# Moving the x tile of the odd groups and the four weight tiles to SBUF addresses that are multiples of 2048 bytes

## The chip, the cores and the metric

The kernel runs on one core of one Trainium2 chip. The metric is the device time of one execution in microseconds; the number to be compared is the median of several runs.

## What is computed

Two stages follow each other. The first is a linear attention with decay, for 4 batches, 8 heads, 768 time steps and a head width of 48:

```python
for t in range(S):
    kt, vt, rt, wt = (k[:, :, t], v[:, :, t], r[:, :, t], w[:, :, t])
    cur = np.einsum('bhd,bhe->bhde', u[None] * kt, vt)
    y[:, :, t] = np.einsum('bhd,bhde->bhe', rt, state + cur)
    state = wt[:, :, :, None] * state + np.einsum('bhd,bhe->bhde', kt, vt)
```

Its output, 3072 tokens of 384 values, goes through a two-layer network with 2048 hidden units; `h`, `g` and the output are in float32:

```python
h = x @ w_in
g = h * (1.0 / (1.0 + np.exp(-1.702 * h)))
return g @ w_out
```

## The kernel before

**Tiling.** The 3072 tokens are 24 chunks of 128. The function `chunk` does the attention of one chunk with small matmuls on TensorE (lines L251, L267, L283, L284, L295, L308, L315) and elementwise work on VectorE and ScalarE. Four chunks make a group of 512 tokens; there are six groups, 0 to 5. The result of a chunk is written, in two parts, into the group's `x` tile: `split` (L192) puts a rounded value (`hi`, L193, ScalarE) and what the rounding lost (`lo`, L194, VectorE). An `x` tile is 128 partitions by 2 parts by 4 blocks of 512 columns in a 4-byte type, so each block is 2048 bytes of every partition and the tile is 16384. Of the four blocks three hold the 384 features; the fourth is a staging block whose rows `fill_x` (L333) copies to their places by DMA.

**The two products.** The weights are kept the same way, as rounded part and rest: `wih`, `wil` for the first layer, `woh`, `wol` for the second, each 128 partitions by 16 hidden slices by 384 columns, 24576 bytes of a partition. A task is one group (or half a group, in group 0) and one of 16 hidden slices `f`. For a task `first_product` does nine matmuls: three feature blocks by three terms, L345 (`wih` with the rounded x), L346 (`wih` with the rest of x) and L347 (`wil` with the rounded x). The weight slice is 128 columns (512 bytes) and is loaded into the array by a LDWEIGHTS of its own; the streamed operand is one block of `x`, 512 columns, read from its first byte to its last. `gelu` turns the sum into `gh` and `gl` (L356 and L357 on ScalarE, L358 on VectorE). `second_product` does nine matmuls likewise: L371 (`woh`, `gh`), L372 (`wol`, `gh`), L373 (`woh`, `gl`), streamed operand `gh` or `gl`, 2048 bytes each. In group 0 most tasks cover 256 columns.

**Order.** The order of everything is written out by hand: `RAMP` and `rest` give a list of tokens, and `do` emits them. In the string, `g`, `h` and `y` stand for first product, gelu and second product of a task; the second product comes two tasks behind the first. The attention of the next chunks is put between the tasks of groups 0 to 4; group 5 has next to none left beside it.

**Where tiles lie.** `new_x` (L383) takes the `x` tile of an even group from the pool `mo` and that of an odd group from the pool `late`:

```python
return (mo if i % 2 == 0 else pools["late"]).tile([P, 2, NP, WIDE], F32R, tag="x", name="x", bufs=1)
```

`late` is opened (L413) when the last weight has been converted, in the memory that the pool `su` with the weights' staging tiles leaves. The pool `cp`, opened first, holds the constants, the four weight tiles, and `acc`, a small tile of sums for a test at the end. The start addresses in each partition, as the program is built, and what is left of them after division by 2048:

```
tile                       bytes    start before  mod 2048
wih, wil, woh, wol         24576 each   22272 ...     1792 (all four)
acc                          240       120576         1792
x of groups 0, 2, 4 (mo)   16384       120832            0
gh (3 buffers), gl (3)      2048 each  141312 ...        0 (all six)
x of groups 1, 3, 5 (late) 16384       194496         1984
rk_t (2 buffers, late)      3072 each  210880      1984, 960
ob (3 buffers, late)        2048 each  217024 ...     1984
```

Since 24576 is 12 times 2048 and a weight slice is 512 bytes, the slices of a weight tile start in turn at 1792, 256, 768 and 1280 mod 2048; one in four runs over a multiple of 2048. Every block of an odd group's `x` starts 64 bytes ahead of a multiple of 2048 and runs over it; no block of an even group's does, and no `gh` or `gl`.

Of the kernel before, what the change touches and what calls it, by code (L numbers as in the profile page):

```python
# [8 lines left out]
F32 = mybir.dt.float32  # L9
F32R = mybir.dt.float32r  # L10
# [9 lines left out]
DM, DFF = H * D, 2048  # L20
NTOK = B * S
P = 128
# [8 lines left out]
NF = DFF // P  # L31
# [44 lines left out]
y38 a13 y39 h40 x11 g41 h41 m12  # L76
"""
WIDE = 512
assert sum(CHUNKS) == NT


@with_exitstack
def rwkv_ffn_kernel(ctx: ExitStack, tc, wkr, vp, vrk, ub, w_in, w_out, masks, vt, uc, out):
# [3 lines left out]
    cp = ctx.enter_context(tc.tile_pool(name="cp", bufs=1))  # L87
# [34 lines left out]

    A.activation(at.tile([P, 1], F32, tag="s", name="junk", bufs=2), after[:, 0:1], AF.Gelu_apprx_sigmoid)

    wih, wil, woh, wol = (cp.tile([P, NF, DM], F32R, name=x) for x in ("wih", "wil", "woh", "wol"))
    acc = cp.tile([P, 2 * NT + 2 * NL], F32, name="acc")
    G.memset(acc, 0.0)

    loaded, state, pools = {}, {}, {}

# [22 lines left out]
    def fetch(i, pool):  # L153

        s, which = divmod(i, 2)
        if s >= NL:
            return
        n = SL // NL
        st = staged[i] = pool.tile([P, n, 2 * NF * DM // SL], I32, tag="st", name="st", bufs=3)
        src = (w_in, w_out)[which][s * n : (s + 1) * n].bitcast(I32)  # L160
        if which == 0:
            for i, (dst, rows) in enumerate(X_ROWS):
                (nc.sync, G)[i % 2].dma_start(st[dst], src[:, rows].rearrange("n p w -> p n w"))
        else:
            nc.sync.dma_start(st, src.rearrange("n p w -> p n w"))

    def convert(i, pool, clamp):

        s, which = divmod(i, 2)
        hi, lo = (wih, wil) if which == 0 else (woh, wol)  # L170
        n = NF * DM // NL
        hi, lo = (x.rearrange("p f m -> p (f m)")[:, s * n : (s + 1) * n] for x in (hi, lo))
        st = staged.pop(i)
        c = pool.tile([P, n], I32, tag="c", name="c", bufs=2)
        w = st.rearrange("p k (n two) -> p (k n) two", two=2)
        l, h = w[:, :, 0], w[:, :, 1]
        cf = c.bitcast(F32)
        sums = {} if clamp else dict(accum_out=acc[:, 2 * NT + i : 2 * NT + i + 1])
        A.activation(l, l.bitcast(U32), AF.Copy, scale=L_SCALE)
        A.activation(cf, h.bitcast(F32), AF.Abs, scale=W_SHIFT, **sums)  # L180
        yield
        V.scalar_tensor_tensor(h, h, -(2 ** 31), l, op0=ALU.bitwise_and, op1=ALU.bitwise_or)
        if clamp:
            V.tensor_scalar(cf, cf, W_MAX, None, op0=ALU.min)
        V.scalar_tensor_tensor(c, c, 3, h, op0=ALU.logical_shift_left, op1=ALU.bitwise_or)
        yield
        A.copy(hi, cf)
        yield
        V.tensor_tensor(lo, cf, hi.bitcast(F32), op=ALU.subtract)  # L189
        yield  # L190
# [136 lines left out]
    def fill_x(x, c0, c1):  # L327

        for m in range(NM):
            for i, dst in enumerate((D, R2)):  # L330
                j = 32 * m + 16 * i
                j += 0 if j < D else HB - D
                (nc.sync, G)[i].dma_start(  # L333
                    x[dst : dst + 16, :, m, c0:c1].bitcast(F32), x[j : j + 16, :, NM, c0:c1].bitcast(F32)
                )
# [3 lines left out]
    def first_product(j, task):  # L339
        i, c0, c1, f = task  # L340
        cs = slice(c0 * C, c1 * C)
        ph = ps_h.tile([P, WIDE], F32, tag="ph", name="ph")[:, 0 : (c1 - c0) * C]
        for c in range(NM):
            h_, l_ = (w[:, f, c * P : (c + 1) * P] for w in (wih, wil))
            T.matmul(ph, h_, xs[i][:, 0, c, cs], start=c == 0, stop=False)  # L345
            T.matmul(ph, h_, xs[i][:, 1, c, cs], start=False, stop=False)  # L346
            T.matmul(ph, l_, xs[i][:, 0, c, cs], start=False, stop=c == NM - 1)  # L347
        parts[j] = ph

    def gelu(j, task):  # L350
        i, c0, c1, f = task
        ph, n = parts[j], (c1 - c0) * C
        gf = mo.tile([P, WIDE], F32, tag="gf", name="gf")[:, 0:n]
        gh = mo.tile([P, WIDE], F32R, tag="gh", name="gh", bufs=LAG + 1)[:, 0:n]
        gl = mo.tile([P, WIDE], F32R, tag="gl", name="gl", bufs=LAG + 1)[:, 0:n]
        A.activation(gh, ph, AF.Gelu_apprx_sigmoid, scale=1.0 / W_SCALE)  # L356
# [4 lines left out]
    def second_product(j, task):  # L361
# [3 lines left out]
        if first:  # L365
            po[i] = [ps_o.tile([P, WIDE], F32, tag=f"po{m}", name=f"po{m}") for m in range(NM)]
        for m in range(NM):
# [7 lines left out]
    def store(i, start, N):  # L375

        for m, o in enumerate(po.pop(i)):
            ob = pools["late"].tile([P, WIDE], F32, tag="ob", name="ob", bufs=3)[:, 0:N]
            A.activation(ob, o[:, 0:N], AF.Copy, scale=1.0 / W_SCALE)
# [7 lines left out]
    with tc.manual_schedule():  # L387
        early = ExitStack()
        su = early.enter_context(tc.tile_pool(name="su", bufs=1))
        where = [(i, col) for i, n in enumerate(CHUNKS) for col in range(n)]  # L390
        starts = [sum(CHUNKS[:i]) for i in range(len(CHUNKS))]
        last = {}
        for j, task in enumerate(TASKS):
            last[task[0]] = j
        running, told = {}, {}

        def piece(kind, i):

            if (kind, i) not in running:
                running[kind, i] = {  # L400
                    "l": load, "a": chunk, "m": measures.get, "w": lambda i: convert(i, su, False)
                }[kind](i)
            next(running[kind, i])

        def do(token):
            kind, i = token[0], int(token[1:] or 0)
            told[token] = told.get(token, 0) + 1
            if kind in "lamw":
                piece(kind, i)
                if kind == "w" and all(told.get(f"w{n}") == 4 for n in range(2 * NL)):  # L410
                    early.close()
                    pools["late"] = fast.enter_context(tc.tile_pool(name="late", bufs=2))
            elif kind == "f":  # L413
                fetch(i, su)
            elif kind == "x":
                group, col = where[i]
                if i == 1:
                    fill_x(xs[group], 0, 2 * C)
                elif i == 3:
                    fill_x(xs[group], 2 * C, 4 * C)  # L420
                elif col == CHUNKS[group] - 1:
                    fill_x(xs[group], 0, (col + 1) * C)
            elif kind == "u":
                nc.sync.dma_start(u_sb, ub)
            elif kind == "M":
                A.dma_start(hm[0:D], masks[0:D])
                A.dma_start(hm[HB:R2], masks[D:R])
            elif kind == "g":
                first_product(i, TASKS[i])
            elif kind == "h":  # L430
                gelu(i, TASKS[i])
            elif kind == "y":
                second_product(i, TASKS[i])
                group = TASKS[i][0]
                if i == last[group]:
                    store(group, starts[group] * C, CHUNKS[group] * C)

        def rest():

            begins = []  # L440
            for t, (i, col) in enumerate(where):
                n = len([x for x in TASKS if x[0] == i - 1])
                begins.append(last.get(i - 1, -1) + 1 - BEFORE - round((CHUNKS[i] - 1 - col) * n / CHUNKS[i]))
            ramp = dict(told)
            for j in range(FIRST, len(TASKS) + LAG):
                for post in range(2):
                    if post and j < len(TASKS):
                        yield f"g{j}"
                        yield f"h{j}"
                    for t, begin in enumerate(begins):  # L450
                        for kind, step, half in PARTS:
                            token = f"{kind}{t + 2 * (kind == 'l')}"
                            if (step + begin, half) > (j, post) or kind == "l" and t + 2 >= NT:
                                continue
                            if ramp.get(token, 0):
                                ramp[token] -= 1
                            elif (step + begin, half) == (j, post):
                                yield token
                if j - LAG >= 0 and f"y{j - LAG}" not in told:
                    yield f"y{j - LAG}"  # L460

        for token in RAMP.split():
            do(token)
        for token in rest():
            do(token)
# [15 lines left out]
    with tc.If(n < full):  # L481
# [5 lines left out]
        with tc.tile_pool(name="gp", bufs=1) as gp, tc.tile_pool(name="ob", bufs=2) as ob, tc.For_i(0, B, 1) as b:  # L487
            pools["late"] = ob
            xg = [new_x(i) for i in range(2)]
            for p in range(NP):  # L490
# [5 lines left out]
                for d in range(D):  # L496
                    rows = []
                    for i, c0 in enumerate((1 + p * CW, 1 + NP * CW + p * C, 1 + NP * CW + NP * C + p * C)):
                        x = gp.tile([R2, CB, C], F32, tag=f"row{i}", name=f"row{i}", bufs=2)
# [16 lines left out]
                for half in range(2):  # L516
                    x = xg[half]
# [65 lines left out]
```

## Time and profile before

| | |
|---|---|
| median of 3 runs | 550.94 us (550.9 to 552.47) |
| profiled execution, first to last instruction | 551.0 us |
| TensorE (matmul) busy | 523.4 us, 95% |
| TensorE weight loads busy | 429.5 us, 78% |
| VectorE, ScalarE busy | 282.8 us, 283.8 us |

The profiled execution's span is taken from the first to the last instruction, and it stands at the median of the timed runs, so sums can be made against either. In the profile PE is the matmul, PEld the weight load, DVE VectorE, ACT ScalarE, POOL GpSimd. Matmuls are pipelined: the next one starts while the last one's result still drains, and the end that the profile gives is modelled. What a matmul costs in a row of them is therefore read from one start to the next, not from its own duration.

### The profile page before, as it was taken

The numbers are of one execution on the slowest core, as the hardware profiler recorded it, in microseconds if no ns is written. First come the engines' busy times: TensorE is split into PE (matmuls) and PEld (weight loads), VectorE is DVE, ScalarE is ACT, GpSimd is POOL, SyncE is SP. The second block draws the span as 40 slices with busy tenths as digits, with TensorE's granted clock in tenths as the row PEclk, the third lists the DMA queues.
The fourth block names the chain that finished last, engine by engine and source line by source line (L and its number), as shares of the span: only waits on it lengthen the run. The fifth ranks groups of instructions, "written<-read, shape, count | busy, mean of one in ns | idle before, by whom it ended". The sixth has DMA issues, their size and how long they took to land.

```text
span 551.0 us, 8703 instructions
## 1 busy us (share of the span) xinstructions
PE 523.4 (95%) x3462; PEld 429.5 (78%) x3462; DVE 282.8 (51%) x438; ACT 283.8 (52%) x616; POOL 32.4 (6%) x69
## 2 busy tenths in 40 slices
PE   2797899999999999999999999999999999999993
PEld 1686799888878778787788777777788787888883
DVE  4898699987636472544544444545445423112110
ACT  2888768876635535555354364444364452332221
POOL 3110200000100001000001000001000001000000
PEclk9958999999999999999999999999999999999997
DMA  9989999243624432134213244223240001000001
GB/s 190 210 167 225 210 210 210 60 94 95 180 50 94 95 93 73 36 117 93 63 32 86 59 130 93 47 49 80 64 131 1 0 1 30 36 23 0 1 0 64
DMA packets 17506, 48.10 MB, mean 87 GB/s; under 512 B 3024, under 2 KB 6416, under 8 KB 17456
## 3 DMA queue, kind: packets, MB, share of 16 engines
q1 hardware_dynamic: 14096, 36.02, 26.2%
q0 software_dynamic: 3104, 11.13, 10.2%
q8 instruction: 29, 0.48, 0.4%
q10 hardware_dynamic: 256, 0.30, 0.2%
q14 instruction: 21, 0.17, 0.1%
HBM read 40.36 MB, written 4.72 MB: 82 GB/s over the span
## 4 chain that ended last, share of the span: by engine, by line
PE 88%; DMA 4%; DVE 3%; ACT 2%; issue 1%; SPq 0%; POOL 0%; DVEq 0%; ACTq 0%
PE po L371 13%; PE ph L345 12%; PE ph L346 12%; PE ph L347 12%; PE po L372 12%; PE po L373 12%; PE ps_s L295 5%; PE ps_y L308 4%; PE ps_y L315 3%; DMA st<-in_w_out 2%; DMA wkr_t<-in_wkr 1%; PE ps_t L267 1%; PE ps_d L251 1%; PE ps_u L283 1%; DMA x<-x 1%
## 5 line engine op out<-in xcount | busy, mean ns | idle before, releaser
L358 DVE TENSOR_TENSOR gl<-gf,gh 128x512 fp32r<-128x512 f32 (+1 forms) x106 | 67.8, 640 | 210.9 <-ACT gf L357 207.4
L356 ACT ACTIVATE gh<-ph 128x512 fp32r<-128x512 f32 (+1 forms) x106 | 59.1, 557 | 193.8 <-PE ph L347 185.2
L345 PE MATMUL ph<-x,wih 128*128 128x512 f32 (+1 forms) x318 | 121.7, 383 | 2.1 <-DMA x<-x 2.1
L371 PE MATMUL po<-gh,woh 128*128 128x512 f32 (+1 forms) x318 | 123.3, 388 | 0.0
L347 PE MATMUL ph<-x,wil 128*128 128x512 f32 (+1 forms) x318 | 119.7, 376 | 0.8 <-DVE wil L189 0.8
L346 PE MATMUL ph<-x,wih 128*128 128x512 f32 (+1 forms) x318 | 119.7, 376 | 0.0
L372 PE MATMUL po<-gh,wol 128*128 128x512 f32 (+1 forms) x318 | 118.0, 371 | 0.0
L373 PE MATMUL po<-gl,woh 128*128 128x512 f32 (+1 forms) x318 | 118.0, 371 | 0.0
L345 PEld LDWEIGHTS ph<-x,wih 128*128 128x128 f32 x318 | 61.3, 193 | 14.7 <-issue 2.7
L371 PEld LDWEIGHTS po<-gh,woh 128*128 128x128 f32 x318 | 60.0, 189 | 14.0 <-issue 2.6
L347 PEld LDWEIGHTS ph<-x,wil 128*128 128x128 f32 x318 | 61.4, 193 | 12.0 <-DVE wil L189 1.0
L346 PEld LDWEIGHTS ph<-x,wih 128*128 128x128 f32 x318 | 61.5, 193 | 10.3
L373 PEld LDWEIGHTS po<-gl,woh 128*128 128x128 f32 x318 | 60.0, 189 | 10.8 <-DVE gl L358 0.2
L372 PEld LDWEIGHTS po<-gh,wol 128*128 128x128 f32 x318 | 60.1, 189 | 8.8
L276 ACT ACTIVATE am<-ident,s 128x128 f32<-128x128 f32 x192 | 58.8, 398 | 7.4 <-PE ps_y L308 5.7
L357 ACT ACTIVATE gf<-ph 128x512 f32<-128x512 f32 (+1 forms) x106 | 58.8, 554 | 0.0
L298 DVE COPY_PREDICATED am<-after,ps_s 128x512 f32<-128x512 int32 x48 | 32.7, 731 | 5.6 <-ACT am L276 3.3
L223 DVE TENSOR_TENSOR_SCAN lp<-wkr_t,d1r 112x516 f32<-112x516 f32 x24 | 29.6, 1232 | 5.7 <-POOL d1r L101 4.2
L295 PE MATMUL ps_s<-kq 48*128 48x128 f32 x384 | 30.6, 298 | 0.6 <-DVE x L194 0.6
L295 PEld LDWEIGHTS ps_s<-kq 48*128 48x128 f32 x384 | 25.6, 199 | 6.3 <-issue 4.7
L308 PE MATMUL ps_y<-am,v_t 128*64 128x128 f32 (+1 forms) x384 | 29.0, 290 | 1.1 <-DVE am L298 1.1
L229 DVE TENSOR_TENSOR_SCAN lp<-wkr_t,d1f 112x516 f32<-112x516 f32 x24 | 29.4, 1225 | 0.1
(62 smaller groups left out, 472.5 us busy)
## 6 DMA issues: line engine op xcount, KB each, us to landing
wkr_t<-in_wkr SPq DMA_DIRECT2D x23, 385.2 KB, 4.7
wkr_t<-in_wkr POOLq DMA_DIRECT2D x23, 288.9 KB, 5.8
st<-in_w_out SPq DMA_DIRECT2D x6, 1024.0 KB, 8.0
rk_t<-in_vrk SPq DMA_DIRECT2D x16, 384.0 KB, 4.6
v_t<-in_vrk SPq DMA_DIRECT2D x24, 192.0 KB, 4.7
out_t<-ob SPq DMA_DIRECT2D x18, 256.0 KB, 2.1
st<-in_w_in POOLq DMA_DIRECT2D x6, 384.0 KB, 9.7
st<-in_w_in SPq DMA_DIRECT2D x6, 384.0 KB, 9.6
```

The source lines that it names most:

```text
L276: A.activation(x_[:, p], ident, AF.Copy, scale=s[:, 2 * p + h : 2 * p + h + 1])
L295: T.matmul(ps[h][:, p], kf[head(h), p], qf[head(h), p], start=True, stop=True)
L308: T.matmul(ps[at_ : at_ + m, p], v_[:, c : c + m], am[h][:, p], start=p == 0, stop=sf is None and p == NP - 1, skip_group_check=True,)
L345: T.matmul(ph, h_, xs[i][:, 0, c, cs], start=c == 0, stop=False)
L346: T.matmul(ph, h_, xs[i][:, 1, c, cs], start=False, stop=False)
L347: T.matmul(ph, l_, xs[i][:, 0, c, cs], start=False, stop=c == NM - 1)
L356: A.activation(gh, ph, AF.Gelu_apprx_sigmoid, scale=1.0 / W_SCALE)
L357: A.activation(gf, ph, AF.Gelu_apprx_sigmoid, scale=1.0 / W_SCALE)
L358: V.tensor_tensor(gl, gf, gh.bitcast(F32), op=ALU.subtract)
L371: T.matmul(o, woh[:, f, ms], gh, start=first, stop=False, skip_group_check=True)
L372: T.matmul(o, wol[:, f, ms], gh, start=False, stop=False, skip_group_check=True)
L373: T.matmul(o, woh[:, f, ms], gl, start=False, stop=f == NF - 1, skip_group_check=True)
```

## The change

`acc` is declared ahead of the four weight tiles in place of behind them, which puts its 240 bytes (and the rounding up to the next tile) ahead of them. When `late` is opened, a tile of 528 columns (2112 bytes) named `pad` is taken from it first, and nothing writes or reads it.

```diff
 WIDE = 512
+PAD = 528
...
-    wih, wil, woh, wol = (cp.tile([P, NF, DM], F32R, name=x) for x in ("wih", "wil", "woh", "wol"))
     acc = cp.tile([P, 2 * NT + 2 * NL], F32, name="acc")
     G.memset(acc, 0.0)
+    wih, wil, woh, wol = (cp.tile([P, NF, DM], F32R, name=x) for x in ("wih", "wil", "woh", "wol"))
...
                     early.close()
                     pools["late"] = fast.enter_context(tc.tile_pool(name="late", bufs=2))
+                    pools["late"].tile([P, PAD], F32, tag="pad", name="pad", bufs=1)
```

The instructions, their order on each engine, and what each waits for are the same before and after. The tiles that move:

```
tile                       start before -> after    mod 2048 before -> after
wih, wil, woh, wol         22272 ... -> 22528 ...   1792 -> 0
acc                        120576 -> 22272          1792 -> 1792
x of groups 1, 3, 5        194496 -> 196608         1984 -> 0
rk_t (2 buffers)           210880, 213952 -> 212992, 216064   1984, 960 -> 0, 1024
ob (3 buffers)             217024 ... -> 219136 ...           1984 -> 0
```

The weight slices then start at 0, 512, 1024 and 1536 mod 2048, and none runs over a multiple of 2048. All other tiles, the even groups' `x`, `gh` and `gl` among them, stay where they are.

## Prediction

> **What bounds the kernel now.** I read the page first: how busy each engine is, over the whole span and by slices.
>
> ```profile
> PE 523.4 (95%) x3462; PEld 429.5 (78%) x3462; DVE 282.8 (51%) x438; ACT 283.8 (52%) x616; POOL 32.4 (6%) x69
> PE   2797899999999999999999999999999999999993
> PEclk9958999999999999999999999999999999999997
> PE 88%; DMA 4%; DVE 3%; ACT 2%; issue 1%; SPq 0%; POOL 0%; DVEq 0%; ACTq 0%
> ```
>
> TensorE is the bound: busy in every slice but the first few and the last, at full clock, and 88% of the chain that ended last. A busy PE can still hide stalls, because its ends are modelled. So I next took the sums by stage, and the waits.
>
> ```profile
> 80.00:120.00 40.00, 40.00 (x348) 36.75 (x347) 35.98 (x53) 32.83 (x69) 1.56 (x3) 1.00 0.54 117
> 420.00:520.00 100.00, 100.00 (x520) 80.69 (x516) 26.37 (x44) 34.42 (x72) 1.53 (x3) 1.00 0.04 13
> PE ps_d L251 <- DVE rku L236: 11.4, 2, 10.3
> PE ph L345 <- DMA x<-x: 2.1, 2, 1.8
> DVE gl L358 <- ACT gf L357: 207.4, 80, 7.2
> ACT gh L356 <- PE ph L347: 185.2, 76, 5.3
> ```
>
> The columns of the first two rows are the window, PE, PEld, DVE, ACT and POOL busy, the clock, and DMA. The waits of TensorE that a row shows are in the start-up; from 80 us on it has none, while VectorE and ScalarE wait for it and for each other, with 207.4 and 185.2 us of idle time ahead of the gelu's steps. A nanosecond taken off a matmul after 80 us is thus a nanosecond off the end, as long as VectorE and ScalarE, idle for almost half of the span, keep up.
>
> The next question is what a matmul costs, and whether the odd groups pay more than the even ones. Two views answer it. The first is the line L345 (the first product, rounded x) in five windows, one for each of groups 1 to 5 in order; the three numbers are the shortest, median and longest duration in ns, and the window of group 1 takes in one matmul of group 2.
>
> ```profile
> L345 PE MATMUL ph<-x,wih x49: 389/395/505, 144.5 to 222.7; 128*128 128x512 f32 x49
> L345 PE MATMUL ph<-x,wih x48: 388/390/395, 222.7 to 302.6; 128*128 128x512 f32 x48
> L345 PE MATMUL ph<-x,wih x48: 393/395/395, 306.1 to 385.9; 128*128 128x512 f32 x48
> L345 PE MATMUL ph<-x,wih x48: 388/389/396, 389.4 to 469.2; 128*128 128x512 f32 x48
> L345 PE MATMUL ph<-x,wih x48: 393/395/395, 471.9 to 535.7; 128*128 128x512 f32 x48
> ```
>
> The medians alternate: 395, 390, 395, 389, 395. Same instruction, same shape, same weights; what alternates is the `x` tile, whose blocks start at 0 mod 2048 in groups 2 and 4 and at 1984 in groups 1, 3 and 5. The second view is the timeline of TensorE, two tasks of group 4 and then two of group 5, in stretches without attention work. Each row is the first of nine matmuls; L345 opens a first product, L371 a second one.
>
> ```profile
> 443.35 0.39 PE L345 MATMUL ph<-x,wih 128*128 128x512 f32 x1
> ...
> 445.39 0.39 PE L371 MATMUL po<-gh,woh 128*128 128x512 f32 x1
> ...
> 447.43 0.39 PE L345 MATMUL ph<-x,wih 128*128 128x512 f32 x1
> ...
> 449.47 0.39 PE L371 MATMUL po<-gh,woh 128*128 128x512 f32 x1
> ```
>
> ```profile
> 492.71 0.40 PE L345 MATMUL ph<-x,wih 128*128 128x512 f32 x1
> ...
> 494.81 0.39 PE L371 MATMUL po<-gh,woh 128*128 128x512 f32 x1
> ...
> 496.87 0.40 PE L345 MATMUL ph<-x,wih 128*128 128x512 f32 x1
> ...
> 498.97 0.39 PE L371 MATMUL po<-gh,woh 128*128 128x512 f32 x1
> ```
>
> In group 4 nine matmuls of a first product take 445.39 - 443.35 = 2.04 us, and again 449.47 - 447.43 = 2.04: 226.7 ns each. In group 5 they take 494.81 - 492.71 = 2.10 and 498.97 - 496.87 = 2.10: 233.3 ns each. The second product, whose streamed operand lies at 0 mod 2048 in all groups, takes 447.43 - 445.39 = 2.04 in group 4 and 496.87 - 494.81 = 2.06 in group 5. So the odd groups' surcharge is 0.06 us per first product, 6.7 ns a matmul, and nearly all of it is in the matmuls that stream `x`.
>
> **The change part by part.** *The x tile of the odd groups.* It reaches 3 groups x 16 tasks = 48 first products of nine matmuls, 432 in all. If the surcharge goes with the start address, each first product falls from 2.10 to 2.04 us: 48 x 0.06 = 2.88 us. The starts are given to 0.01 us, so a single reading of 0.06 can be off by 0.01; that it repeats narrows this. The lower bound is the difference of the durations, 395 - 389.5 = 5.5 ns: 432 x 5.5 = 2.4 us. The upper bound adds the 0.02 us by which the second product was longer in group 5: 48 x 0.08 = 3.84 us; but that operand and the place where it lies do not change, so I count none of it. Between the two I take 2.8 us, near the start-to-start reading and pulled slightly to the durations. All of it is on the path: in groups 1 and 3 attention work stands between the tasks, on the same TensorE, in a fixed order, and the gelu steps have the idle time quoted above as cover. If that cover were gone, the matmuls of the next task would wait for `gl`; with each task shortened by 0.06 of about 4.1 us, 1.5%, and VectorE and ScalarE at half their time, it is not.
>
> [...]
>
> *The four weight tiles.* They change what LDWEIGHTS reads, 128 columns for every one of the 1908 product matmuls. The load lies beside the running matmul:
>
> ```profile
> L345 PEld LDWEIGHTS ph<-x,wih x48: 187/188/188, 389.2 to 469.0; 128*128 128x128 f32 x48
> ```
>
> These are the 48 loads of group 4, over all 16 slices and three blocks, hence twelve from each of the four starts 1792, 256, 768 and 1280 mod 2048, a quarter of which run over a multiple of 2048. They take 187 to 188 ns without exception: a load that runs over the boundary is not longer by more than 1 ns. And at 188 ns a load fits under a matmul's 226.7 with 38 ns to spare. So this part is worth nothing, and its cover is that slack. Its bounds come from the matmuls themselves; here is group 4 again by mean duration, and the counts of one line over the whole run.
>
> ```profile
> L345 PE MATMUL ph<-x,wih 128*128 128x512 f32 x48 | 18.7, 390 | 0.0
> ```
>
> ```profile
> L371 PE MATMUL po<-gh,woh 128*128 128x512 f32 x258 | 106.0, 411 | 0.0
> L371 PE MATMUL po<-gh,woh 128*128 128x256 f32 x60 | 17.3, 288 | 0.0
> ```
>
> The mean of the 48 is 390 ns and the shortest 388, so what the four weight starts cost on average is under 2 ns a matmul and, with the median at 389, more likely 1 at most: 1 ns on the 1548 full matmuls, 1.5 us either way, as the far end. (Each of the six lines L345 to L347 and L371 to L373 has 258 matmuls of 512 columns, 1548 in all, and 60 of 256 columns, 360 in all.)
>
> *acc, rk_t, ob, pad.* `pad` emits nothing. `acc` is set once at the start and read at the end by small VectorE work. `rk_t` is landed by DMA and multiplied on VectorE; `ob` is written by ScalarE and stored by DMA. Of all these only the last `ob` steps lie on the path, behind the last matmul:
>
> ```profile
> 542.07 1.28 ACT L379 ACTIVATE ob<-po 128x512 f32<-128x512 f32 x2
> ```
>
> 1.28 us for two, 0.6 us each, does not hang on an address as far as this row shows; I put 0, with 0.1 us either way.
>
> Sum: 551.0 - 2.8 = 548.2 by the span, and 550.94 - 2.8 = 548.1 us against the median of the runs.
>
> **The rivals.** *No change.* The surcharge belongs to something else that odd groups share: the tile lies at the top of the memory, above the staging tiles and the outputs' `ob`, and still does. For it: before, "misaligned" and "in the pool late" are the same three groups, and no full-width matmul streams a misaligned tile elsewhere. Against it: nothing runs beside group 5 that could disturb that region, and the surcharge is as constant there (393 to 395) as in group 3. Time 551.0. [...] Chance 0.08.
>
> *Slower.* Once the weights start at the same remainder as the streamed operand (0 mod 2048), weight load and streaming meet in the same part of the memory and wait for each other. Before, no weight slice shared its start with `x`, `gh` or `gl`; after, one in four does, in all groups. At the same 6.7 ns, a quarter of 1908 pays 477 x 6.7 = 3.2 us, which gives 551.3 after the 2.8; if all pay, 12.8 us and 560.9. It decides as soon as over 432 of the 1908 matmuls pay. Against it: four different distances between weight start and `x` start exist today in group 4, and four more in the odd groups, and none stands out in the narrow ranges 388 to 396 and 393 to 395. Chance 0.04.
>
> *Much faster.* Something in the 226.7 ns itself comes from the weights' start, which is 256 mod 512 for all slices before and 0 after. The array streams 512 columns; the rows with 256 columns do not tell what a column costs alone. If the weights gave back another 6.7 ns for each of the 1548 full matmuls, 10.4 us, the time would be 537.7. Against it: the load is hidden with 38 ns to spare. Chance 0.03. [...]
>
> **How the numbers follow.** The forecast, the x term alone, has 0.85 and gives 548.1. Its bounds are 3.84 us saved with nothing else, 547.1, and 2.4 us saved with 0.5 us lost in the weights or to the spread of the runs, 549.0. The runs shown lie between 550.9 and 552.47, so a median of few can stand somewhat high; I set the range from 547.0 to 549.6. Left out are no change (0.08), the slower case (0.04), the much faster one (0.03) and a few hundredths of the forecast's own tails. A measurement of this kernel can tell about 0.3%, 1.65 us, from no change. Faster by more than that means below 549.3: the forecast nearly whole and the much faster case, 0.87. Within 0.3%: no change, half of the slower case, and a forecast halved, 0.10. Slower: 0.03.
>
> **What would show it.** In the changed kernel L345, L346 and L347 should have the same median in all five windows, 389 or 390, and nine matmuls of a first product in group 5 should take 2.04 us in place of 2.10; L371 to L373 and the even groups should be as now, and the weight loads at 188. If L345 of group 5 stays at 395, the address was not the cause. If even groups rise above 389, weights and streamed operand meet. If the loads stay at 188 and all matmuls fall below 226.7, the weights' start counted after all. If the matmuls come out as said but the end does not move by 48 x 0.06, some wait of TensorE on gelu or attention has taken the place, and the list of waits after 80 us would name it.

## The result and the profile after

| | before | after |
|---|---|---|
| median, 7 runs each | 551.09 us (550.09 to 553.51) | 548.43 us (545.92 to 549.88) |
| ratio, 95% interval | | 0.9935 (0.9914 to 0.9956) |
| profiled execution, first to last instruction | 551.0 us | 544.3 us |
| TensorE matmul busy | 523.4 us | 521.7 us |

The change saves 2.66 us by the medians. The ratio is that of the means, 548.06 to 551.64, which is 3.6 us; its interval allows 2.4 to 4.7. The two profiled executions differ by 6.7 us, which is more than the kernels do. The span leaves out about 1.6 us of an execution: the run whose span is 544.3 took 545.92, and that is the fastest of its seven. By the same 1.6 us the profiled execution before, with its span of 551.0, took some 552.6 and does not stand at the median, as I had it ahead of the prediction; sums against the span are about 1.6 us off, differences are not. And 3.1 of the 6.7 us lie ahead of group 1. Here are windows of the start-up of the kernel after (length, then PE, PEld, DVE, ACT and POOL busy, clock, DMA share, GB/s):

```profile
20.00:40.00 20.00, 18.85 (x139) 16.10 (x139) 19.35 (x28) 16.29 (x35) 2.56 (x5) 1.00 0.89 189
40.00:60.00 20.00, 18.59 (x165) 17.07 (x164) 16.82 (x23) 16.72 (x37) 1.05 (x2) 0.91 1.02 224
60.00:80.00 20.00, 20.00 (x170) 20.00 (x169) 16.77 (x22) 16.60 (x31) 4.67 (x9) 1.00 0.92 211
```

and the same of the kernel before:

```profile
20.00:40.00 20.00, 17.67 (x143) 15.10 (x142) 19.76 (x28) 16.58 (x35) 2.56 (x5) 0.66 0.93 194
40.00:60.00 20.00, 17.20 (x170) 15.04 (x170) 16.82 (x24) 17.12 (x37) 1.06 (x2) 0.91 0.98 221
60.00:80.00 20.00, 17.89 (x136) 17.55 (x135) 14.20 (x19) 13.42 (x26) 4.67 (x9) 0.91 0.96 216
```

In the start-up, where TensorE still waits for other engines and for DMAs (in the kernel before 11.4 us on VectorE's `rku` and 2.1 us on the DMA of `x`, in the kernel after 11.3 us on `rku`), the granted clock was 0.66 from 20 to 40 us in the execution before and 1.00 in the one after, and group 1 began at 144.5 us in the one and at 141.4 in the other. That is how single executions differ, not how the kernels do: with the odd x tile alone moved (below) group 1 began at 145.3 us, and in another execution of the kernel after at 143.3. So the change is read from group 1 on. Its line in five windows, one for each of groups 1 to 5 (L346 here is L345 of the kernel before):

```profile
L346 PE MATMUL ph<-x,wih x49: 389/389/501, 141.4 to 218.7; 128*128 128x512 f32 x49
L346 PE MATMUL ph<-x,wih x48: 389/389/389, 218.7 to 298.6; 128*128 128x512 f32 x48
L346 PE MATMUL ph<-x,wih x48: 389/389/389, 302.1 to 380.8; 128*128 128x512 f32 x48
L346 PE MATMUL ph<-x,wih x48: 389/389/395, 384.3 to 464.0; 128*128 128x512 f32 x48
L346 PE MATMUL ph<-x,wih x48: 389/389/389, 466.7 to 529.3; 128*128 128x512 f32 x48
```

The alternation of 395 and 389 is gone: 389 in every group. From the first of these matmuls in group 1 to the last in group 5 it was 535.7 - 144.5 = 391.2 us before and is 529.3 - 141.4 = 387.9 now, 3.3 us less. (The two times in these rows are the first and the last start.) In the timeline of group 5, the first of nine matmuls in each row:

```profile
499.38 0.39 PE L346 MATMUL ph<-x,wih 128*128 128x512 f32 x1
...
501.42 0.39 PE L372 MATMUL po<-gh,woh 128*128 128x512 f32 x1
...
503.46 0.39 PE L346 MATMUL ph<-x,wih 128*128 128x512 f32 x1
```

First product 2.04 us, where it was 2.10; second product 2.04, where it was 2.06, though nothing that it reads from `gh` and `gl` moved.

### The profile page after: what moved, and what is told of

Read it like the earlier page. It is cut to its first block, busy times and chain, and to the rows that moved or that the text cites. A ratio compares the mean times of both kernels' runs of the same rounds, so it can differ in the third digit from the quotient of the medians.

```text
span 544.3 us, 8703 instructions
## 1 busy us (share of the span) xinstructions
PE 521.7 (96%) x3462; PEld 431.8 (79%) x3462; DVE 282.4 (52%) x438; ACT 284.0 (52%) x616; POOL 32.4 (6%) x69
## 4 chain that ended last, share of the span: by engine, by line
PE 89%; DMA 2%; DVE 1%; ACT 1%; SPq 0%; issue 0%
PE po L372 14%; PE ph L346 12%; PE po L374 12%; PE po L373 12%; PE ph L348 12%; PE ph L347 12%; PE ps_s L296 4%; PE ps_y L309 4%; PE ps_y L316 3%; DMA st<-in_w_out 2%; PE ps_u L284 1%; PE ps_t L268 1%; PE ps_d L252 1%; PE ps_u L285 1%; SPq L334 0%; DVE st L183 0%
## 5 line engine op out<-in xcount | busy, mean ns | idle before, releaser
L346 PE MATMUL ph<-x,wih 128*128 128x512 f32 (+1 forms) x318 | 120.3, 378 | 0.0
L347 PE MATMUL ph<-x,wih 128*128 128x512 f32 (+1 forms) x318 | 118.6, 373 | 0.0
L346 PEld LDWEIGHTS ph<-x,wih 128*128 128x128 f32 x318 | 61.1, 192 | 11.2 <-issue 1.0
L296 PE MATMUL ps_s<-kq 48*128 48x128 f32 x384 | 31.8, 304 | 0.0
## 6 DMA issues: line engine op xcount, KB each, us to landing
st<-in_w_in SPq DMA_DIRECT2D x6, 384.0 KB, 11.4
```

The lines of the kernel that those rows point to most:

```text
L296: T.matmul(ps[h][:, p], kf[head(h), p], qf[head(h), p], start=True, stop=True)
```

## The experiments

All twelve kernels have the instructions, order and waits of the kernel after; only addresses differ, and the diffs are against it. Numbers "from start to start" without a row are means over a trace's timeline, of the matmuls of 512 columns that have another product matmul ahead of them and behind; in group 5 those are 143 or 144 for each product. The stretch from the first start of the first product's line in group 1 to its last in group 5 is quoted as "the stretch": 391.2 us before, 387.9 after, and 387.9 again in the second execution of the kernel after, although that began group 1 1.9 us later.

**The change in its parts.** The kernel after again, on the chip of the next three:

> The changed kernel as it is, beside its parts on the same chip. Every theory: 0.993 to 0.996 of the kernel before, first-product matmuls of all groups 226.7 ns from start to start.

Measured: 547.87 us, ratio 0.9934 (0.9908 to 0.9959).

Then the pad alone, with the order of `acc` and the weights as before:

```diff
-    acc = cp.tile([P, 2 * NT + 2 * NL], F32, name="acc")
-    G.memset(acc, 0.0)
     wih, wil, woh, wol = (...)
+    acc = cp.tile([P, 2 * NT + 2 * NL], F32, name="acc")
+    G.memset(acc, 0.0)
```

> Only the pad: the odd groups' x at 0 mod 2048, the four weight tiles back at 1792. Theory (the streamed operand's start alone counts): the odd groups' first product falls from 233.3 to 226.7 ns a matmul, the whole gain of 2.8 us is here, ratio 0.995. Rival (the weights' start counts, or both must match): no more than half of it, ratio 0.9975 or above. Open: whether the second product of the odd groups, which fell from 228.6 to 226.7 ns in group 5 with both parts, falls here too; by the theory it reads nothing that the pad moves, and stays at 228.6.

Measured: 548.42 us, ratio 0.9935 (0.9911 to 0.9958). Group 5 of its timeline:

```profile
503.23 0.39 PE L346 MATMUL ph<-x,wih 128*128 128x512 f32 x1
...
505.27 0.39 PE L372 MATMUL po<-gh,woh 128*128 128x512 f32 x1
...
507.31 0.39 PE L346 MATMUL ph<-x,wih 128*128 128x512 f32 x1
```

2.04 and 2.04 us, and the stretch is 533.1 - 145.3 = 387.8 us:

```profile
L346 PE MATMUL ph<-x,wih x240: 388/389/501, 145.3 to 533.1; 128*128 128x512 f32 x120
```

The whole gain is in the x tile, and so is the second product's 0.02 us: that it would stay was wrong. And the weights alone:

```diff
-                    pools["late"].tile([P, PAD], F32, tag="pad", name="pad", bufs=1)
```

> Only the order of acc and the weights: weights at 0 mod 2048, the odd groups' x back at 1984. Theory: first products as before, 233.3 ns in odd groups and 226.7 in even ones, time within 0.2% of before, except for what the second product gives (at most 0.7 us). Rival (the weights' start counts): a gain of half of the 2.7 us or more, ratio 0.9975 or below, with the odd groups' first product under 231 ns.

Measured: 550.85 us, ratio 0.9986 (0.9970 to 1.0002), and group 5 as in the kernel before, 2.10 and 2.06 us:

```profile
503.91 0.39 PE L346 MATMUL ph<-x,wih 128*128 128x512 f32 x1
...
506.01 0.39 PE L372 MATMUL po<-gh,woh 128*128 128x512 f32 x1
...
508.07 0.39 PE L346 MATMUL ph<-x,wih 128*128 128x512 f32 x1
```

The stretch is 534.4 - 143.3 = 391.1 us, that of the kernel before within 0.1:

```profile
L346 PE MATMUL ph<-x,wih x240: 388/394/504, 143.3 to 534.4; 128*128 128x512 f32 x120
```

**The cost put where it was not.** The pool of the even groups' x, `gh` and `gl`, 64 bytes up:

```diff
     mo = ctx.enter_context(tc.tile_pool(name="mo", bufs=2))
+    mo.tile([P, 16], F32, tag="shift", name="shift", bufs=1)
...
-PAD = 528
+PAD = 512
```

> The changed kernel, with the pool of the even groups' x, gf, gh and gl moved up by 64 bytes (x of the odd groups and the weights stay at 0 mod 2048): the cost put where it was not. Theory (a streamed operand that starts off a multiple of 2048 pays 6.5 ns): the even groups' first products and all second products of 512 columns rise from 226.7 to 233.3 ns, 342 first and 774 second matmuls, 1116 x 6.5 = 7.3 us, so 1.009 of the kernel before. Rival (the place in memory, not the start, made the odd groups slow): no change against both parts, 0.995. In group 0 the 256-column matmuls read 1024 bytes at 64 and at 1088 mod 2048, the first within a block of 2048 and the second over its end: if running over the end is what costs, only the second kind rises from 120 ns; if the start's remainder costs, both do.

Measured: 550.36 us, ratio 0.9982 (0.9967 to 0.9998); 2.5 us slower than the kernel after on the same chip, where 7.3 were expected. Group 4, where now every streamed operand is off:

```profile
440.59 0.39 PE L347 MATMUL ph<-x,wih 128*128 128x512 f32 x1
...
442.65 0.39 PE L373 MATMUL po<-gh,woh 128*128 128x512 f32 x1
...
444.71 0.39 PE L347 MATMUL ph<-x,wih 128*128 128x512 f32 x1
```

2.06 us each in place of 2.04, 2 ns a matmul and not 6.5. The tile that was moved got slower where it stands, which speaks against the place in memory; but the price of a start at 64 mod 2048 among others at 64 is not that of 1984. Nor did the cost stay with what was moved. In group 5 x and the weights still start at 0 mod 2048, and only `gh` and `gl` are off:

```profile
506.63 0.40 PE L347 MATMUL ph<-x,wih 128*128 128x512 f32 x1
...
508.71 0.40 PE L373 MATMUL po<-gh,woh 128*128 128x512 f32 x1
...
510.78 0.40 PE L347 MATMUL ph<-x,wih 128*128 128x512 f32 x1
```

2.08 and 2.07 us here; over the whole group 231.6 ns for the first product, which reads nothing that moved, and 229.0 for the second, where the kernel after has 226.7 for both. The aligned matmuls lost 5 ns, more than the shifted ones between them. So a matmul's pace does not follow from its own operands' starts alone, and no run shows by what path its neighbours' starts reach it. The 256-column matmuls of group 0 did not rise in either half of a block: their median from start to start went from 120 to 118 ns.

**Which starts cost.** Three kernels spread the odd groups' blocks out, so that one execution has up to six different starts:

```diff
+        wide = WIDE if i % 2 == 0 else WIDE + STEP
-        return (...).tile([P, 2, NP, WIDE], F32R, tag="x", name="x", bufs=1)
+        return (...).tile([P, 2, NP, wide], F32R, tag="x", name="x", bufs=1)[:, :, :, 0:WIDE]
```

with `STEP` 16, 64 and 4 and `PAD` 16. These kernels, and those below for which no ratio is given, were timed once; seven executions of the kernel after lie 4 us apart, so they are read by their traces and not by their times.

> The odd groups' x begins at 194560 (0 mod 2048, below the 196608 of the changed kernel) and its blocks stand 2112 bytes apart in place of 2048, so the six that are streamed start at 0, 64, 128 (rounded part) and 256, 320, 384 (rest) mod 2048, all in one run. If running over a multiple of 2048 costs: 226.7 ns at 0 and 233.3 at the other five. If a start off 128 costs: 233.3 at 64 and 320 alone. If the place costs (194560 is 64 bytes above the tile's place before): 233.3 at all six.

Measured, group 5, the first of three matmuls in each row (one block of features each):

```profile
504.30 0.39 PE L347 MATMUL ph<-x,wih 128*128 128x512 f32 x1
...
504.98 0.40 PE L347 MATMUL ph<-x,wih 128*128 128x512 f32 x1
...
505.68 0.40 PE L347 MATMUL ph<-x,wih 128*128 128x512 f32 x1
...
506.38 0.39 PE L373 MATMUL po<-gh,woh 128*128 128x512 f32 x1
...
508.45 0.39 PE L347 MATMUL ph<-x,wih 128*128 128x512 f32 x1
```

The first block, with starts at 0 and 256, takes 0.68 us, three at 226.7 ns; the blocks at 64 and 320 and at 128 and 384 take 0.70 each. The start at 256 runs over a multiple of 2048 and costs nothing, 128 costs: the unit is not 2048, and a multiple of 128 is not enough. One execution of this kernel took 551.47 us, beside 550.48 of the kernel before.

> As with steps of 64, blocks 2304 bytes apart: starts at 0, 256, 512 (rounded part) and 1024, 1280, 1536 (rest). If running over a multiple of 2048 costs: 226.7 at 0, 233.3 at the other five. If only starts off 128 or 256 cost: 226.7 at all six. If the cost grows with the distance from a multiple of 2048: largest at 1024.

Measured, group 5, nine matmuls ahead of each of the later two rows:

```profile
502.70 0.39 PE L347 MATMUL ph<-x,wih 128*128 128x512 f32 x1
...
504.74 0.39 PE L373 MATMUL po<-gh,woh 128*128 128x512 f32 x1
...
506.78 0.39 PE L347 MATMUL ph<-x,wih 128*128 128x512 f32 x1
```

2.04 us and 2.04: all six starts, 0, 256, 512, 1024, 1280 and 1536 mod 2048, are at 226.7 ns, and in every odd group the means agree with those of the kernel after within 0.2 ns. A multiple of 256 was enough here, where all other operands started at one too. (549.36 us in one execution, 550.48 before.)

> As before, blocks 2064 bytes apart: starts at 0, 16, 32 (rounded part) and 64, 80, 96 (rest). If running over a multiple of 2048 costs a fixed time: 226.7 at 0 and 233.3 at the other five. [...]

Measured: 231.2 ns on average over group 5's first products, where a fixed cost at all starts but 0 (seven of the nine matmuls) would give 231.8. The single values go from 225 to 241 ns, and the two matmuls of the first block that both start at 0 stand at 226.9 and 241.0; starts mixed so finely can't be priced one by one. (548.69 us in one execution, 550.48 before.)

So I gave each group one start of its own, with rows of 576 columns in both x tiles:

```diff
+FROM = {2: 16, 3: 32, 4: 48, 5: 63}
...
+        at0 = FROM.get(i, 0)
+        x = (...).tile([P, 2, NP, WIDE + 64], F32R, tag="x", name="x", bufs=1)
+        return x[:, :, :, at0 : at0 + WIDE]
```

> All blocks of one group start at the same remainder, another one in each group: both x tiles have rows of 576 columns (blocks 2304 bytes apart, a multiple of 256, which cost nothing before) and a group streams them from a column of its own. Start mod 256: group 1: 0, group 2: 64, group 3: 128, group 4: 192, group 5: 252. Theory now (what counts is the start mod 256; the fewer bytes there are up to the next multiple of 256, the more is lost): first product 226.7 ns in group 1's quiet tasks, about 228.5 in group 2, more in group 3, 233.3 in group 4 (as the kernel before has it at 1984, 192 mod 256), and most in group 5. Rival (any start off a multiple of 256 costs the same 6.5 ns): 233.3 in groups 2 to 5.

> As the run with starts 64 to 252; starts mod 256 here: group 1: 0, group 2: 16, group 3: 32, group 4: 224, group 5: 4. Theory (short way to the next multiple of 256 costs): groups 2, 3 and 5 below 228.5 ns, group 4 above 233.3. Rival (every start off a multiple of 256 costs the same): 233.3 in groups 2 to 5.

The second has `FROM = {2: 4, 3: 8, 4: 56, 5: 1}`. Measured, mean ns from start to start, and what the second product of the same group took above the kernel after (the column of 0 is the kernel after, without its group 1, which stands at 228.4). Each other column is one group of one execution, with the weights, `gh` and `gl` at multiples of 256:

```
start mod 256    0      4     16     32     64    128    192    224    252
group            2-5    5      2      3      2      3      4      4      5
first product  226.7  236.2  231.6  233.7  231.1  232.4  233.2  233.6  227.0
second, more     0     +0.7   +2.4   +2.0   +0.6   +2.0   +1.6   +0.7   +1.0
```

The column of 192 is a group 4, whose tile lies in the pool `mo`:

```profile
444.44 0.39 PE L347 MATMUL ph<-x,wih 128*128 128x512 f32 x1
...
446.54 0.39 PE L373 MATMUL po<-gh,woh 128*128 128x512 f32 x1
...
448.60 0.39 PE L347 MATMUL ph<-x,wih 128*128 128x512 f32 x1
```

2.10 and 2.06 us: with the remainder that the odd groups had before (1984 is 192 mod 256), a tile in the other pool takes what theirs took, while group 1 of the same run, in the pool `late` at 0, takes what it takes in the kernel after. That settles it against the place.

Group 5 with its start 4 bytes behind a multiple of 256, nine matmuls from row to row:

```profile
504.99 0.40 PE L347 MATMUL ph<-x,wih 128*128 128x512 f32 x1
...
507.11 0.40 PE L373 MATMUL po<-gh,woh 128*128 128x512 f32 x1
...
509.16 0.40 PE L347 MATMUL ph<-x,wih 128*128 128x512 f32 x1
```

2.12 us, the slowest of all starts, and 252 almost free: both the opposite of "the shorter the way to the next multiple, the more is lost", and "the same everywhere" fails as well. What makes the one start cost 4 ns and the other 10 stays open. (553.07 and 552.51 us in single executions, 551.12 before.)

**The weights off 256.** 22272, where the weights began before, is 87 times 256. The change had moved them from one multiple of 256 to another.

```diff
+    cp.tile([P, 16], F32, name="ahead")
     wih, wil, woh, wol = (...)
+    cp.tile([P, 48], F32, name="behind")
...
-PAD = 528
+PAD = 464
```

> The changed kernel with the weights at 64 mod 2048 in place of 0; the pool of the even groups' x, gh and gl goes up by 256 bytes, the odd groups' x stays. The weights stood at 1792 before, which is a multiple of 256 already, so the run with the weights alone could not tell whether a start off 256 costs a load. Theory (the load is hidden under the streaming): matmuls at 226.7 ns as in the changed kernel, whatever the load takes. Rival (a weight load off 256 holds the array as a streamed operand does): loads longer than 188 ns and matmuls above 229 ns in all groups, some 5 us in all.

Measured: 556.12 us in one execution, 551.12 for the kernel before on that chip. Group 5, with nine matmuls from row to row:

```profile
508.71 0.40 PE L348 MATMUL ph<-x,wih 128*128 128x512 f32 x1
...
510.81 0.39 PE L374 MATMUL po<-gh,woh 128*128 128x512 f32 x1
...
512.91 0.40 PE L348 MATMUL ph<-x,wih 128*128 128x512 f32 x1
```

and its weight loads there:

```profile
L348 PEld LDWEIGHTS ph<-x,wih x19: 188/188/189, 508.5 to 533.7; 128*128 128x128 f32 x19
```

Both products take 2.10 us, 233.1 to 233.6 ns a matmul on average in all groups, while a recorded load still takes 188 ns. The cover that the theory counted on does not exist: what the load's start costs shows in the matmul's pace, although the load's own record does not show it.

**Both off at once.** The same kernel without the pad, so that the odd x is at 192 mod 256 again.

> The run with the weights at 64 mod 256, and without the pad, so the odd groups' x stands at 192 mod 256 again, as before the change. In the odd groups' first product both what is loaded and what is streamed is off a multiple of 256. If each pays for itself (both fetches take turns at something): 226.7 + 6.6 + 6.5, about 240 ns from start to start in group 5. If they run side by side and the longer one decides: 233.3 ns, as with either alone. Second products and even groups at 233.3 by both.

Measured, group 5:

```profile
506.62 0.39 PE L348 MATMUL ph<-x,wih 128*128 128x512 f32 x1
...
508.71 0.39 PE L374 MATMUL po<-gh,woh 128*128 128x512 f32 x1
...
510.81 0.39 PE L348 MATMUL ph<-x,wih 128*128 128x512 f32 x1
```

2.09 and 2.10 us, 231.9 and 233.3 ns on average: not 240. The two costs are not added to each other. Left open is whether each start counts by itself or how far the two lie apart: no run has weights and streamed operand at one and the same remainder other than 0 mod 256. (554.16 us in one execution, 552.93 before.)

**The attention's tiles at multiples of 256.** Rows of `wkr_t`, `lp`, `junk` and `s` rounded up, `PAD` 64:

```diff
-        lp = at.tile([R2, 2 * n], F32, tag="lp", name="lp")
+        lp = at.tile([R2, 1088], F32, tag="lp", name="lp")[:, 0 : 2 * n]
```

> The changed kernel with the attention's tiles (lp, rku, kq, kt, am, sf, s and the loads wkr_t, v_t) at multiples of 256 as well; kq stood at 160, am, kt and sf at 192, v_t at 64 mod 256; the odd groups' x goes to 196096, 1536 mod 2048. If the attention's matmuls pay like the products': up to 3 us off 24 chunks of three lines of eight pairs (576 pairs at some 6 ns). Theory: they are paced by the weight loads, pairs at 103 to 107 ns, and gain nothing: 0.994 of the kernel before, as the changed kernel.

Measured: 547.07 us, ratio 0.9931 (0.9910 to 0.9951). That can't be told from the kernel after, 0.9935. The attention's lines with the tiles moved:

```profile
L296 PE MATMUL ps_s<-kq 48*128 48x128 f32 x384 | 31.4, 304 | 0.4 <-DVE x L195 0.4
L309 PE MATMUL ps_y<-am,v_t 128*64 128x128 f32 x192 | 28.2, 291 | 1.1 <-DVE am L299 1.1
L316 PE MATMUL ps_y<-kq,sf 48*48 48x128 f32 x320 | 22.1, 278 | 0.0
```

and in the kernel after:

```profile
L296 PE MATMUL ps_s<-kq 48*128 48x128 f32 x384 | 31.8, 304 | 0.0
L309 PE MATMUL ps_y<-am,v_t 128*64 128x128 f32 x192 | 28.3, 292 | 0.5 <-DVE am L299 0.5
L316 PE MATMUL ps_y<-kq,sf 48*48 48x128 f32 x320 | 22.4, 281 | 0.0
```

304 and 304, 291 and 292, 278 and 281 ns. These are durations, whose ends are modelled (the products' matmuls are recorded at 0.39 us each and start 0.23 us apart); the stretch, which holds the attention of some 16 of the 24 chunks, is the better measure:

```profile
L346 PE MATMUL ph<-x,wih x240: 389/389/501, 142.6 to 530.7; 128*128 128x512 f32 x120
```

530.7 - 142.6 = 388.1 us, where the kernel after has 387.9. Moving these tiles gained nothing.

## Why the prediction was right, and where its steps were not

*TensorE sets the end.* Right: no wait of it stands after 80 us in the two profiled executions (a second one of the kernel after has a single wait of 1.3 us on the gelu between 80 and 100 us, still in group 0), and what the matmuls lost, the stretch from group 1 to group 5 lost: the means from start to start, times 144 for each product and group, fell by 3.4 us, the stretch by 3.3.

*The x term, 2.8 us.* Right in place and about right in size: 3.3 us in the profiled stretch, 2.66 by the medians, 3.6 by the means. By the trace two errors partly cancel in it: the odd groups' first products gave 2.6 us and not 2.8, since group 1 lost 4.9 ns a matmul where groups 3 and 5 lost 6.5 and 6.7, and the second products gave 0.75 us that the sum had at nothing. That the medians come within 0.2 us of 2.8 is luck, as the runs scatter by 4 us. The step "that operand and the place where it lies do not change, so I count none of it" failed: the second product's 0.02 us went too, and it went with the x tile alone. In group 5 a task fell from 4.16 to 4.08 us, 16 x 0.08 = 1.3 us there; in groups 1 and 3, between attention work, it was less. Why a matmul that reads aligned operands is longer beside some that don't, no run settles; that it is so, the kernel with the shifted pool shows again, with 231.6 ns in its group 5.

*The weight tiles, nothing.* The number was right and its reason wrong. I wrote that the load fits under a matmul with 38 ns to spare and that this slack is the cover. With the weights at 64 mod 256 the loads still took 188 ns and the matmuls of group 5 6.4 to 7 ns more, some 8 us from group 1 on by the means. As far as the runs show, the part was worth nothing because the weights stood at a multiple of 256 before and after. The four starts that I compared, 1792, 256, 768 and 1280, are all multiples of 256 too: the view could not have shown the cost, and I took its silence for a proof.

*The other tiles, nothing.* Nothing measured speaks against it; weights alone, with `acc` moved, gave 0.9986 (0.9970 to 1.0002), and the stretch was 391.1 us for 391.2.

*No change, because of the place.* Refuted: with blocks from 194560 on, 64 bytes above the old place, starts at multiples of 256 are at 226.7 ns, and a tile of an even group, in the other pool, took 233.2 ns at 192 mod 256.

*Slower, weights and stream at one remainder.* Refuted: with weights, x, `gh` and `gl` at 0 mod 2048 the first products of groups 2 to 5 take 226.7 ns, group 1 takes 228.4 where it took 233.3, and no second product got slower.

*Much faster.* Refuted: with everything at 0 mod 2048 the 226.7 ns stayed. No run has a group whose mean lies below 226.5 ns for 512 columns.

## What to carry to other kernels

Where matmuls of 512 four-byte columns follow each other without a gap, put everything that is streamed or loaded in that stretch at SBUF addresses that are multiples of 256 bytes; 2048 wasn't needed here (226.7 ns at all six starts of the kernel with steps of 256), a start off 256 cost up to 10 ns of 227 (236.2 at 4 bytes), and matmuls that were aligned themselves paid for others that were not (231.6 ns in group 5 of the kernel with the shifted pool). With 256 columns no such cost showed: 118 and 117 ns from start to start with a start off 256, for 120. Look for it by comparing one line's start-to-start time over tiles that differ in nothing but their address, and see that the tiles compared really differ in the remainder that counts. A load that was hidden by its record, 188 ns under a matmul's 226.7, was on the path all the same (233.3 ns a matmul with the weights at 64 mod 256), so a move of the weights is priced by the matmul's pace and not by the load's slack.

## What was not expected of the hardware

- A weight load that starts 64 bytes past a multiple of 256 takes the recorded 188 ns, as an aligned one does, and the matmuls go from 226.7 to 233.3 ns with it.
- Streamed and loaded operand off 256 together cost no more than one of them: 231.9 and not 240 ns.
- The price of a start is not monotone: 236.2 ns at 4 bytes past a multiple of 256, 231.1 at 64, 233.6 at 224, 227.0 at 252; and with all streamed operands at 64 it is 228.7.
- Behind nine matmuls that stream an operand off 256, the next nine, aligned ones are longer on average: by up to 2.4 ns where x is off, and by 5 ns in group 5 of the kernel whose `gh` and `gl` are off.
- Matmuls of 256 columns got faster, not slower: a median of 118 ns from start to start in place of 120 with their streamed operands at 64 mod 256, and of 117 with their weights there.
